# Half-width attention matmuls from one head's block, and a weight sign set on ScalarE

## The chip, the cores and the metric

The kernel runs on one core of a Trainium2 chip. The metric is the device time of one execution in microseconds (us). Three runs of the kernel before took 496.63, 497.72 and 499.42 us; the median is 497.72 us.

Engines are named as the profile names them: PE is TensorE's matmul stream and PEld its weight loads, DVE is VectorE, ACT is ScalarE, POOL is GpSimd, SP is SyncE, which here issues all DMAs.

## The reference

A linear attention over 8 batches of 8 heads, 576 positions and 64 dimensions a head, feeds a feed-forward layer with a softmax-gated unit and a layer norm:

```python
q_s = exp(q - max(q, axis=-1));  q_s /= sum(q_s, axis=-1) + 1e-09
k_s = exp(k - max(k, axis=2));   k_s /= sum(k_s, axis=2) + 1e-09
kv = einsum('bhsd,bhse->bhde', k_s, v)          # 64 x 64 for each head
x = einsum('bhsd,bhde->bhse', q_s, kv)          # -> (4608, 512)
h = x @ w_in                                     # (4608, 1024)
sm = exp(h - max(h));  sm /= sum(sm) + 1e-09
solu = h * sm
ln = (solu - mean(solu)) / sqrt(var(solu) + 1e-06) * g_ln
out = ln @ w_out                                 # (4608, 512)
```

The weights and g_ln come as 64-bit floats, w_in with 512 x 1024 and w_out with 1024 x 512 elements.

## The kernel before, in words

**Tiles.** The 4608 rows are cut into 36 row tiles of 128: each batch has 4 tiles of its 512 main rows, and the last 64 rows of two batches share one tile, called a rest tile here. A tile goes through three works: attend (`x`, kv against q gives x transposed), hidden (`h`, x against w_in, then the softmax unit) and project (`o`, against w_out). In the works' names the number is the tile's, in the tensors' names it is batch and tile of the batch: `x1_0` is batch 1, first tile.

**Two parts.** Operands of the f16 matmuls are held as a high f16 part and a low f16 part (what the high part misses). `three` (L474) multiplies high by high, high by low and low by high into one f32 accumulator. `hidden` (L515) issues 24 matmuls of 512 columns a tile at L526, `project` (L587) 24 at L600, each the same three products.

**Attention.** `keys` (L335) takes the maxima of k on DVE, turns them on PE (L322, L329), subtracts and exponentiates, and forms kv with f32 matmuls (L376, L381): 64 columns wide, alternating between the two heads of a pair, whose results lie in accumulator partitions 0 to 63 and 64 to 127. Then kv is normalised, scaled by a power of two and written into `bd` (L128): for each pair of heads a 128 x 128 block with head 0's 64 x 64 block and head 1's on the diagonal and zeros elsewhere, once for the high part (L399, ACT) and once for the low part (L401, DVE). `queries` (L441) and `rest_queries` (L463) compute q's softmax; `parts` gives the high and the low part's places in `qhl`, where each part holds all heads in a row, and a DMA transposes both into `qT`: for each part and pair a 128 x 128 block. `attend` (L493) issues, for each of 4 pairs, three matmuls of 128 x 128 weights and 128 columns (L475 to L477), 12 a tile; a rest tile has two batches' halves with 64 columns each, 24 matmuls.

**Weights.** `float_of` (L230) makes f32 from the 64-bit words: ACT scales the high word as a float (L237, Copy), DVE shifts it left by 3 and masks the sign off (L239), ors the low word's upper bits in (L241), and ors the sign of the high word in (L243). It runs eight times over 128 x 1024 elements: four for w_in (`iw`, works w0 to w3), four for w_out (`gw`, y0 to y3). The works W and Z then scale the weights to `wi` (L268, L270) and `wo` (L309, L311); `h` needs `wi`, `o` needs `wo`.

**Order.** The kernel is written as generators. `ORDER`, a long string, says which work makes its next step; a letter behind a dot (`.v`, `.p`, `.a`) moves that step to DVE, POOL or ACT. As all steps are issued in this order, the string sets each engine's queue, SP's DMA queue among them. In front stand the loads, K0, Q0, the weights and some `P` steps (`warm_up`, L648: idle matmuls on `bd[2]`).

Of the kernel before, what the change touches and what calls it, by code (L numbers as in the profile page):

```python
# [83 lines left out]
)  # L84


@with_exitstack
def linear_attention_solu_ffn(ctx: ExitStack, tc: tile.TileContext, q, k, v, w_in, w_out, g_ln, out):

# [35 lines left out]
    vr = cst.tile([P, H, D + 1], F32, name="vr")  # L125
    nc.vector.memset(vm[:, :, :, D : D + 1], 1.0)
    nc.vector.memset(vr[:, :, D : D + 1], 1.0)
    bd = [cst.tile([P, 2, NP, P], F16, name=f"bd{i}") for i in range(3)]  # L128
    for t in reversed(bd):
        nc.gpsimd.memset(t, 0.0)  # L130

# [309 lines left out]
    def queries(b, c0, c1):  # L441
# [5 lines left out]
        def parts():  # L447
            if c0 % 2 == 0:
                hl_of[b] = sb.tile([P, 2, 2, H, D], F16, name=f"qhl{b}_{c0}", tag="qhl", bufs=1)
            if n == 1:  # L450
                return (hl_of[b][:, c0 % 2, i] for i in range(2))
# [268 lines left out]
```

## Time and profile before

| what | value |
|---|---|
| median of three runs | 497.72 us |
| the profiled execution's own time | 498.03 us |
| its span, first to last instruction | 496.2 us |
| mean granted TensorE clock | 0.968 |
| `h` matmuls, L526 | 864, busy 206.0 us |
| `o` matmuls, L600 | 888, busy 197.7 us |
| `x` matmuls, L475 to L477 | 128 in each line of 128 columns, 32 in each of 64 columns |
| `kv` matmuls, L376 and L381 | 512 and 128 records |
| DMA | 74.98 MB, mean 151 GB/s |

How to read the profile: busy shares are shares of the span; the lengths of matmuls overlap, so what a matmul takes of PE's stream is read from the distance of starts. A slice row has 40 digits, each the busy share of a fortieth of the span in tenths. A row of windows gives a stretch, then for each engine its busy time and number of instructions, then the granted clock, the DMA share and GB/s. A row of groups gives line, engine, operation, tensors, shape, count, busy time and mean length of one in ns, then idle time ahead and who ended it. A row of the timeline gives start and length in us; brackets hold the idle time ahead and its releaser.

### The profile page before, as it was taken

The page shows a single profiled execution, that of the slowest core. Times are in us where ns is not written, and L with a number is a line of the kernel's source. Part 1 is how long each engine was busy: PE and PEld are TensorE (multiplying, and loading weights), DVE is VectorE, ACT ScalarE, POOL GpSimd, SP SyncE. Part 2 cuts the span into 40 slices and gives each one's busy share as a digit, 9 for nine tenths or more (in the row PEclk, how much of TensorE's full clock was granted, in tenths as well). Part 3 has the DMA queues.
Part 4 walks back from the last instruction along what each step waited for, and adds up shares of the span by engine and source line. Part 5 has one row for each costly group of instructions (what it writes and reads, how often), then busy time and mean ns, then how long its engine had stood idle before and what let it go on. Part 6 is the DMA issues. An engine that isn't in the chain of part 4 may idle for free.

```text
span 496.2 us, 8006 instructions
## 1 busy us (share of the span) xinstructions
PE 456.0 (92%) x2994; PEld 232.4 (47%) x2994; DVE 370.2 (75%) x606; ACT 278.5 (56%) x457; POOL 207.4 (42%) x305
## 2 busy tenths in 40 slices
PE   7456774999999999999999989999999999999997
PEld 2314441445554545554555444555554554444444
DVE  4999989989888679888876897779874654635330
ACT  1747588676756665684565455734764644533320
POOL 3540578358855643833276262515115320122200
PEclk9777987999999999999999999999999999999999
DMA  8596968439896599749967954684544554150532
GB/s 278 201 241 189 292 171 198 106 76 234 195 218 150 129 195 175 156 107 204 217 135 147 247 117 99 180 199 118 127 108 80 112 86 101 27 128 3 126 107 63
DMA packets 159239, 74.98 MB, mean 151 GB/s; under 512 B 127840, under 2 KB 152672, under 8 KB 159200
## 3 DMA queue, kind: packets, MB, share of 16 engines
q1 hardware_dynamic: 159200, 74.47, 65.0%
q8 instruction: 23, 0.38, 0.3%
q14 instruction: 16, 0.13, 0.1%
HBM read 36.70 MB, written 9.44 MB: 93 GB/s over the span
## 4 chain that ended last, share of the span: by engine, by line
PE 73%; DVE 19%; issue 3%; ACT 2%; DMA 1%; POOL 1%; SPq 0%; DVEq 0%; ACTq 0%; POOLq 0%
PE o L600 32%; PE h L526 32%; PE kv L376 3%; DVE u L562 2%; DVE iw L241 1%; DVE qnmx L418 1%; DMA qm<-in_q_dram 1%; PE x L475 1%; PE x L476 1%; PE x L477 1%; DVE h L555 1%; DVE wo L311 1%; DVE top L533 1%; ACT u L560 1%; DVE gw L241 1%
## 5 line engine op out<-in xcount | busy, mean ns | idle before, releaser
L526 PE MATMUL h<-wi,xT 128*128 128x512 f16 x864 | 206.0, 386 | 9.0 <-ACT e L569 8.7
L600 PE MATMUL o<-wo,uT 128*128 128x512 f16 (+1 forms) x888 | 197.7, 373 | 2.6 <-ACT os L610 1.4
L526 PEld LDWEIGHTS <-xT 128*128 128x128 f16 x864 | 84.3, 99 | 106.2 <-issue 16.2
L600 PEld LDWEIGHTS <-uT 128*128 128x128 f16 x888 | 86.2, 98 | 99.7 <-issue 3.4
L533 DVE TENSOR_REDUCE top<-h 128x1 f32<-128x1024 f32 x36 | 43.8, 1217 | 20.9 <-PE h L526 20.5
L562 DVE SCALAR_TENSOR_TENSOR u<-h,nmu,u 128x1024 f16<-128x1024 f32 x36 | 45.9, 1276 | 14.4 <-ACT u L560 14.1
L569 ACT ACTIVATE e<-h,nmu 128x1024 f32<-128x1024 f32 x36 | 39.9, 1110 | 26.7 <-DVE u L562 26.6
L555 DVE SCALAR_TENSOR_TENSOR h<-h,ph,e 128x1024 f32<-128x1024 f32 x36 | 46.4, 1289 | 8.1 <-POOL ph L552 5.2
L549 POOL TENSOR_TENSOR p<-pi,mone 128x1 f32<-128x1 f32 x36 | 23.4, 651 | 55.3 <-DVE pi L546 54.3
L535 ACT ACTIVATE nm<-top,hs 128x1 f32<-128x1 f32 x32 | 9.4, 294 | 61.0 <-DVE top L533 61.0
L543 POOL TENSOR_SCALAR am<-nm 128x1 f32<-128x1 f32 x23 | 9.5, 413 | 77.9 <-ACT nm L535 77.7
L560 ACT ACTIVATE u<-h,nmu 128x1024 f16<-128x1024 f32 x36 | 40.0, 1112 | 0.9
L539 ACT ACTIVATE e<-h,nm,hs 128x1024 f32<-128x1024 f32 x32 | 38.4, 1202 | 0.9
L608 DVE TENSOR_SCALAR os<-o,rr 128x512 f32<-128x512 f32 (+1 forms) x17 | 12.2, 717 | 31.9 <-PE o L600 31.9
L431 POOL TENSOR_TENSOR qm<-qm,qrec 128x1024 f32<-128x1024 f32 (+1 forms) x13 | 24.8, 1907 | 14.3 <-DVE qrec L429 11.3
L557 ACT ACTIVATE nmu<-s 128x1 f32<-128x1 f32 x36 | 7.3, 202 | 40.6 <-DVE h L555 39.5
L420 POOL TENSOR_TENSOR qm<-qm,qnmx 128x1024 f32<-128x1024 f32 (+1 forms) x13 | 25.6, 1969 | 8.7 <-DVE qnmx L418 8.5
L436 POOL TENSOR_TENSOR qhl<-qm,qhl 128x1024 f16<-128x1024 f32 (+1 forms) x11 | 21.6, 1963 | 17.7 <-DVE qhl L149 13.0
L511 DVE SCALAR_TENSOR_TENSOR xT<-x,xT 128x512 f16<-128x512 f32 x36 | 24.5, 680 | 4.4 <-ACT xT L509 4.3
L610 ACT ACTIVATE os<-o,rr 128x512 f32<-128x512 f32 x20 | 13.7, 685 | 23.1 <-PE o L600 13.7
L475 PE MATMUL x<-qT,bd 128*128 128x128 f16 x128 | 24.0, 225 | 2.2 <-DVE col L325 2.1
L582 POOL TENSOR_TENSOR r<-var,mhalf 128x1 f32<-128x1 f32 x36 | 20.1, 562 | 14.0 <-DVE var L579 13.2
(137 smaller groups left out, 657.4 us busy)
## 6 DMA issues: line engine op xcount, KB each, us to landing
v<-in_v_dram SPq DMA_DIRECT2D x32, 256.0 KB, 3.7
out_dram<-os SPq DMA_DIRECT2D x31, 256.0 KB, 3.4
km<-in_k_dram SPq DMA_DIRECT2D x7, 1024.0 KB, 6.9
qm<-in_q_dram SPq DMA_DIRECT2D x7, 1024.0 KB, 7.4
w_in<-in_moe_w_in_dram SPq DMA_DIRECT2D x8, 512.0 KB, 7.1
w_out<-in_moe_w_out_dram SPq DMA_DIRECT2D x8, 512.0 KB, 4.4
out_dram<-os SPq DMA_DIRECT2D x10, 128.0 KB, 2.4
km<-in_k_dram SPq DMA_DIRECT2D x2, 512.0 KB, 4.5
```

Source lines behind the costliest of these rows:

```text
L420: on(nc.gpsimd).tensor_tensor(x, x, wide(nmx), op=ALU.add)
L431: on(nc.gpsimd).tensor_tensor(x, x, wide(rec), op=ALU.mult)
L475: nc.tensor.matmul(acc, ah, bh, start=True, stop=False)
L511: nc.vector.scalar_tensor_tensor(xT[:, 1], acc, 1.0 / QS, xT[:, 0], op0=ALU.mult, op1=ALU.subtract)
L526: nc.tensor.matmul(h[:, ns], xT[:, t, kc], wi[:, s, kc, ns], start=(i == 0), stop=(i == len(terms) - 1))
L533: nc.vector.tensor_reduce(top, h, axis=AX.X, op=ALU.max, negate=True)
L539: nc.scalar.activation(e, h, AF.Exp, bias=nm, scale=hs, accum_out=z)
L555: nc.vector.scalar_tensor_tensor(h, h, ph, e, op0=ALU.mult, op1=ALU.mult, accum_out=s1)
L560: nc.scalar.activation(u[:, 0], h, AF.Identity, bias=nmu)
L562: nc.vector.scalar_tensor_tensor(u[:, 1], h, nmu, u[:, 0], op0=ALU.add, op1=ALU.subtract)
L569: nc.scalar.activation(e, h, AF.Square, bias=nmu, accum_out=s2)
L600: nc.tensor.matmul(o, uT[:, j, f], wo[:, s, f, cols], start=(f == 0 and j == 0 and s == 0), stop=(f == NF - 1 and j == 1))
```

## The change

Four things change.

1. `bd` is [128, 2, 8 heads, 64] instead of pairs of 128 x 128. For each head, slot 0 holds kv's high part in partitions 0 to 63 and again in 64 to 127 (ACT writes one half and copies it to the other), slot 1 holds the low part in partitions 0 to 63 and zeros below.
2. In `qhl` the high and the low part of one head lie side by side (64 and 64), so that the transposed `qT` holds for each head the high part in partitions 0 to 63 and the low part in 64 to 127. `attend` issues for each head two matmuls with 64 columns of weights: 16 a tile instead of 12, the two heads of a pair in turn; a rest tile has 32 instead of 24. `three` is gone.
3. The first pass of `float_of` is Prelu with a slope of -2^32 instead of Copy: a negative input comes out positive with its exponent raised by 32, which the shift by 3 turns into the sign bit. The mask and the sign pass (L243 before) are gone: two DVE passes instead of three.
4. `ORDER` is another string.

```diff
 ORDER = (
-    "LK0*4 LQ0 K0*4 LQ0 K0 P*4 K0*2 w3 Q0c w3 K0*4 V00 w3 Q0a Q0a.v V03 V00 K0.v w0*2 Q0a Q0c V01 K0 Q0b "
...
+    "LQ0*2 LK0*3 V03 w3 Q0a K0*4 Q0a*2 K0 P*4 K0 Q0b w3 V00 V03.v K0 Q0c K0 Q0b Q0a w3 w0 K0 w3 V00 Q0b "
...
-    bd = [cst.tile([P, 2, NP, P], F16, name=f"bd{i}") for i in range(3)]
+    bd = [cst.tile([P, 2, H, D], F16, name=f"bd{i}") for i in range(3)]
...
-        nc.scalar.activation(x, high.bitcast(F32), AF.Copy, scale=2.0**-112)
-        yield
-        nc.vector.tensor_scalar(xi, xi, 3, 0x7FFFFFFF, op0=ALU.logical_shift_left, op1=ALU.bitwise_and)
+        nc.scalar.activation(x, high.bitcast(F32), AF.Prelu, scale=2.0**-112, alpha=-(2.0**32))
+        yield
+        nc.vector.tensor_scalar(xi, xi, 3, -1, op0=ALU.logical_shift_left, op1=ALU.bitwise_and)
         yield
         nc.vector.scalar_tensor_tensor(xi, low, 29, xi, op0=ALU.logical_shift_right, op1=ALU.bitwise_or)
-        yield
-        nc.vector.scalar_tensor_tensor(xi, high, -0x80000000, xi, op0=ALU.bitwise_and, op1=ALU.bitwise_or)
         yield
...
+        places = t.rearrange("p s (n j) d -> p s n j d", j=2)
         for i in range(2):
-            hp = slice(i * D, (i + 1) * D)
-            nc.scalar.activation(t[hp, 0, :, hp], kvn[hp], AF.Copy, scale=s[hp])
+            hp, other = slice(i * D, (i + 1) * D), slice((1 - i) * D, (2 - i) * D)
+            high = places[:, 0, :, i]
+            nc.scalar.activation(high[hp], kvn[hp], AF.Copy, scale=s[hp])
+            yield
+            nc.scalar.copy(high[other], high[hp])
             yield
             nc.vector.scalar_tensor_tensor(
-                t[hp, 1, :, hp], kvn[hp], s[hp], t[hp, 0, :, hp], op0=ALU.mult, op1=ALU.subtract
+                places[0:D, 1, :, i], kvn[hp], s[hp], high[hp], op0=ALU.mult, op1=ALU.subtract
             )
...
-                hl_of[b] = sb.tile([P, 2, 2, H, D], F16, name=f"qhl{b}_{c0}", tag="qhl", bufs=1)
+                hl_of[b] = sb.tile([P, 2, H, 2, D], F16, name=f"qhl{b}_{c0}", tag="qhl", bufs=1)
...
-            out=qT_of[b, c0][:, cs].rearrange("p c t n k -> p (c t n) k"),
-            in_=hl_of[b][:, cs].rearrange("p c t h d -> p (c t h d)"),
+            out=qT_of[b, c0][:, cs].rearrange("p c h k -> p (c h) k"),
+            in_=hl_of[b][:, cs].rearrange("p c h t d -> p (c h t d)"),
...
             for pr in range(NP):
-                three(acc[:, pr, cols], t[:, 0, pr], t[:, 1, pr], qT[:, 0, pr, cols], qT[:, 1, pr, cols])
+
+                for s in range(2):
+                    for j in range(2):
+                        nc.tensor.matmul(
+                            acc[j * D : (j + 1) * D, pr, cols], t[:, s, 2 * pr + j], qT[:, 2 * pr + j, cols],
+                            start=(s == 0), stop=(s == 1),
+                        )
```

Three places of the new order, as the built programs hold it. First DVE's queue where `wo` is made, before:

```order
L304 TENSOR_SCALAR gs_806<-gl_69,s_out_803 128x8
L401 SCALAR_TENSOR_TENSOR bd1_81<-kvn1_698,s_kv1_759,bd1_81 64x4x64
L346 TENSOR_TENSOR khalf2_819<-km2_737 128x512
L311 SCALAR_TENSOR_TENSOR wo_68<-gw0_451,gs_806,wo_68 128x512 x2
L311 SCALAR_TENSOR_TENSOR wo_68<-gw1_480,gs_806,wo_68 128x512 x2
L311 SCALAR_TENSOR_TENSOR wo_68<-gw2_594,gs_806,wo_68 128x512
L511 SCALAR_TENSOR_TENSOR xT1_1_853<-x1_1_840,xT1_1_853 128x512
```

and the same place now:

```order
L304 TENSOR_SCALAR gs_841<-gl_69,s_out_838 128x8
L348 TENSOR_TENSOR ktop2_828<-khalf2_829 128x256
L518 SCALAR_TENSOR_TENSOR xT1_1_826<-x1_1_807,xT1_1_826 128x512
L311 SCALAR_TENSOR_TENSOR wo_68<-gw0_444,gs_841,wo_68 128x512
L346 TENSOR_TENSOR khalf2_829<-km2_736 128x512
L424 TENSOR_REDUCE qnmxr0_853<-qr0_623 128x8
L311 SCALAR_TENSOR_TENSOR wo_68<-gw0_444,gs_841,wo_68 128x512
L311 SCALAR_TENSOR_TENSOR wo_68<-gw1_504,gs_841,wo_68 128x512 x2
```

The low part of batch 1's first x (`xT1_1`) stood behind five `wo` passes and stands ahead of all now; a khalf and a row maximum of q's rest stand between the first two `wo` passes. Next PE's queue ahead of the first `o` matmul, before (`x1_0` is batch 1's first tile; the rows are the last of its 12 matmuls with their weight loads):

```order
L476 LDWEIGHTS bd1_81
L476 MATMUL x1_0_858<-qT1_0_740,bd1_81 128x128
L477 LDWEIGHTS bd1_81
L477 MATMUL x1_0_858<-qT1_0_740,bd1_81 128x128
L600 LDWEIGHTS uT0_0_562
L600 MATMUL o0_00_891<-wo_68,uT0_0_562 128x512
```

and now the same tile's 16, with what stands around them (rows that read alike are left out at the marks):

```order
L533 LDWEIGHTS xT1_1_826
L533 MATMUL h1_1_876<-wi_67,xT1_1_826 128x512
L509 LDWEIGHTS bd1_81
L509 MATMUL x1_0_885<-qT1_0_732,bd1_81 64x128
...
L533 LDWEIGHTS xT1_1_826
L533 MATMUL h1_1_876<-wi_67,xT1_1_826 128x512
...
L607 LDWEIGHTS uT0_0_569
L607 MATMUL o0_00_912<-wo_68,uT0_0_569 128x512
```

Four `h` matmuls of `h1_1` stand ahead of this tile and four behind it, and only then comes the first `o`: eight `h` matmuls moved ahead of it. Last SP's queue at the program's start, before:

```order
L181 DMA km0_97<-in_k_dram 128x4x256 x2
L200 DMA kr0_100<-in_k_dram 64x8x64
L181 DMA qm0_102<-in_q_dram 128x4x256 x2
L227 DMA w_in3_139<-in_moe_w_in_dram 128x1024 x2
L187 DMA v0_0_153<-in_v_dram 128x2x256
```

and now:

```order
L182 DMA qm0_97<-in_q_dram 128x4x256 x2
L182 DMA km0_100<-in_k_dram 128x4x256 x2
L201 DMA kr0_103<-in_k_dram 64x8x64
L188 DMA v0_3_105<-in_v_dram 128x2x256
L228 DMA w_in3_107<-in_moe_w_in_dram 128x1024 x2
```

q's two halves now go ahead of k's, and one block of v ahead of the first weights.

More of the change, by code (lines that the diff above doesn't have):

```diff
@@ L448, in parts @@
             if c0 % 2 == 0:
-                hl_of[b] = sb.tile([P, 2, 2, H, D], F16, name=f"qhl{b}_{c0}", tag="qhl", bufs=1)
+                hl_of[b] = sb.tile([P, 2, H, 2, D], F16, name=f"qhl{b}_{c0}", tag="qhl", bufs=1)
             if n == 1:
-                return (hl_of[b][:, c0 % 2, i] for i in range(2))
-            return (hl_of[b][:, :, i].rearrange("p c h d -> p h c d") for i in range(2))
+                return (hl_of[b][:, c0 % 2, :, i] for i in range(2))
+            return (hl_of[b][:, :, :, i].rearrange("p c h d -> p h c d") for i in range(2))
         yield from q_softmax(x[:, :, 0] if n == 1 else x, parts, H * n, f"{b}_{c0}")
         if c0 % 2 == 0:
-            qT_of[b, c0] = sb.tile([P, 2, 2, NP, P], F16, name=f"qT{b}_{c0}", tag="qT", bufs=2)
+            qT_of[b, c0] = sb.tile([P, 2, H, P], F16, name=f"qT{b}_{c0}", tag="qT", bufs=2)
             qT_of[b, c0 + 1] = qT_of[b, c0]
         nc.sync.dma_start_transpose(
-            out=qT_of[b, c0][:, cs].rearrange("p c t n k -> p (c t n) k"),
-            in_=hl_of[b][:, cs].rearrange("p c t h d -> p (c t h d)"),
+            out=qT_of[b, c0][:, cs].rearrange("p c h k -> p (c h) k"),
+            in_=hl_of[b][:, cs].rearrange("p c h t d -> p (c h t d)"),
         )
@@ L464, in parts @@
         def parts():
-            hl_of["rest"] = sb.tile([P, 2, H, D], F16, name=f"qhlr{b}", tag="qhlr", bufs=1)
-            return (hl_of["rest"][:, i] for i in range(2))
+            hl_of["rest"] = sb.tile([P, H, 2, D], F16, name=f"qhlr{b}", tag="qhlr", bufs=1)
+            return (hl_of["rest"][:, :, i] for i in range(2))
         yield from q_softmax(raw["qr"], parts, H, f"r{b}")
-        qT = qT_of["rest", b // 2] = sb.tile([P, 2, NP, P], F16, name=f"qTr{b}", tag="qTr", bufs=1)
+        qT = qT_of["rest", b // 2] = sb.tile([P, H, P], F16, name=f"qTr{b}", tag="qTr", bufs=1)
         nc.sync.dma_start_transpose(
-            out=qT.rearrange("p t n k -> p (t n) k"), in_=hl_of["rest"].rearrange("p t h d -> p (t h d)")
+            out=qT, in_=hl_of["rest"].rearrange("p h t d -> p (h t d)")
         )
-    def three(acc, ah, al, bh, bl):
-        nc.tensor.matmul(acc, ah, bh, start=True, stop=False)
-        nc.tensor.matmul(acc, ah, bl, start=False, stop=False)
-        nc.tensor.matmul(acc, al, bh, start=False, stop=True)
     xT_of, uT_of, r_of, hs_of = {}, {}, {}, {}
@@ L648, in warm_up @@
     def warm_up():
-        idle = bd[2][:, 0].rearrange("p n k -> p (n k)")
+        idle = bd[2][:, 0].rearrange("p h d -> p (h d)")
         while True:
@@ L654, in warm_up @@
             for _ in range(4):
-                nc.tensor.matmul(acc, bd[2][:, 0, 0], idle, start=True, stop=True)
+                nc.tensor.matmul(acc, idle[:, 0:P], idle, start=True, stop=True)
             yield
```

124 rows, old and new, of the table ORDER are left out of this document.

## The prediction

> **What bounds the kernel now.** I read the page's busy rows and the two slice rows first, then the windows of two stretches, then the timeline where the one stretch passes into the other.
>
> ```profile
> span 496.2 us, 8006 instructions
> PE 456.0 (92%) x2994; PEld 232.4 (47%) x2994; DVE 370.2 (75%) x606; ACT 278.5 (56%) x457; POOL 207.4 (42%) x305
> PE   7456774999999999999999989999999999999997
> DVE  4999989989888679888876897779874654635330
> ...
> 10.00:92.00 82.00, 51.33 (x377) 27.50 (x378) 78.08 (x109) 57.47 (x88) 44.22 (x41) 0.81 0.78 218
> 92.00:493.00 401.00, 397.51 (x2597) 202.43 (x2596) 287.97 (x488) 219.55 (x368) 159.82 (x256) 1.00 0.63 136
> ```
>
> The 92% of PE is an average over two kernels in one. From 10 to 92 us PE works 51 of 82 us and DVE 78.1 of 82: DVE's queue is the clock there. From 92 to 493 us PE is busy 397.5 of 401 us at a granted clock of 1.00, and DVE 288: PE is the clock. So an edit is worth what it takes off DVE's queue in the first stretch and off PE's stream in the second; anything else must only not be late.
>
> ```profile
> 89.73 5.04 DVE L311 SCALAR_TENSOR_TENSOR wo<-gw,gs,wo 128x512 f16<-128x512 f32 x5
> 91.16 0.38 PE L600 MATMUL o<-wo,uT 128*128 128x512 f16 x1
> 92.17 2.58 PE L600 MATMUL o<-wo,uT 128*128 128x512 f16 x11 [0.63 <-DVE wo L311]
> ```
>
> This is the hand-over: the first `o` matmuls start at 91.16 and then wait for DVE's second `wo` pass. From there PE runs to the end, so the kernel ends when the second `wo` pass is done plus PE's remaining stream.
>
> **First stretch: DVE's queue ahead of the second wo pass.** The change takes the sign pass away (L243, eight times), since ScalarE's pass sets the sign. The new order also carries other passes across this point. Counted in the order of both kernels, up to the second `wo` pass: gone are the eight sign passes, one half-size qm+qnmx and one qhl subtraction. New are two copies into vm, one half-size cast, one khalf, one ktop, one km-kb, two full qm·qrec and one half-size one, one xT, and three 128x1 passes.
>
> ```profile
> L243 DVE SCALAR_TENSOR_TENSOR iw<-w_in,iw 128x1024 int32<-128x1024 int32 x4 | 4.9, 1225 | 0.1
> L243 DVE SCALAR_TENSOR_TENSOR gw<-w_out,gw 128x1024 int32<-128x1024 int32 x4 | 4.8, 1216 | 0.0
> L420 DVE TENSOR_TENSOR qm<-qm,qnmx 128x512 f32<-128x512 f32 x1 | 2.0, 1983 | 0.0
> L436 DVE TENSOR_TENSOR qhl<-qm,qhl 128x1024 f16<-128x1024 f32 x6 | 7.6, 1271 | 0.3 <-ACT qhl L147 0.3
> ...
> L149 DVE COPY vm<-v x4: 414/654/2317, 195.7 to 346.7; 128x512 f32<-128x512 f32 x4
> L149 DVE CAST qhlr<-qr 128x512 f16<-128x512 f32 x1 | 0.4, 417 | 0.0
> L346 DVE TENSOR_TENSOR khalf<-km 128x512 f32<-128x512 f32 x16 | 13.2, 826 | 4.6 <-DMA km<-in_k_dram 4.3
> L348 DVE TENSOR_TENSOR ktop<-khalf 128x256 f32<-128x256 f32 x16 | 8.1, 505 | 0.3
> L357 DVE TENSOR_TENSOR km<-km,kb 128x1024 f32<-128x1024 f32 x8 | 10.7, 1337 | 2.2 <-ACT kb L332 2.2
> L431 DVE TENSOR_TENSOR qm<-qm,qrec 128x1024 f32<-128x1024 f32 x4 | 4.9, 1220 | 0.1
> L511 DVE SCALAR_TENSOR_TENSOR xT<-x,xT 128x512 f16<-128x512 f32 x36 | 24.5, 680 | 4.4 <-ACT xT L509 4.3
> L552 DVE TENSOR_TENSOR ph<-p,hs 128x1 f32<-128x1 f32 x14 | 3.9, 278 | 3.1 <-POOL p L549 3.1
> ```
>
> Gone: 4 x 1.225 + 4 x 1.216 = 9.76, with 1.98 and 1.27 more it is 13.0 us. New: 2 x 0.65 (the median of the vm copies; their ends are 0.41 and 2.32) + 0.42 + 0.83 + 0.51 + 1.34 + 2 x 1.22 + 0.61 (half of 1.22) + 0.68 + 3 x 0.28 = 9.0 us. **Net -4.0 us.** With the copies at 0.41 it is -4.5, at 2.32 it is -0.7; were all of what moved hidden, the sign passes alone would give -9.8. I take -4.0, since DVE has no idle time here that could swallow it.
>
> ScalarE's pass is Prelu instead of Copy; its length is not in the trace. The two nearest rows, L237's own and Exp over the same size, bound it at 1.05 to 1.13 us; as ScalarE is busy 57 of 82 us, that is nothing. The copy that each head half of kv now makes on ScalarE is not in the trace either: between nothing and the 0.50 us of L399, which handles the same 64x256; I take 0.5. Two stand ahead of each batch's first `x`. DVE's low pass waits only for the activation ahead of each copy, as before, so one copy at most lies on the path to `x`; PE's `h` and `o` of the batch before cover it. With that cover gone it would be 0.5 us in each of 8 batches, 4 us.
>
> ```profile
> L237 ACT ACTIVATE gw<-w_out 128x1024 f32<-128x1024 f32 x4 | 4.5, 1126 | 0.0
> L422 ACT ACTIVATE qm<-qm 128x1024 f32<-128x1024 f32 x15 | 15.8, 1053 | 1.0 <-POOL qm L420 1.0
> L399 ACT ACTIVATE bd<-kvn,s_kv 64x256 f16<-64x256 f32 x16 | 8.0, 500 | 1.8 <-DVE s_kv L167 1.6
> ...
> 4.61 0.69 DVE L346 TENSOR_TENSOR khalf<-km 128x512 f32<-128x512 f32 x1 [3.63 <-DMA km<-in_k_dram]
> 7.64 0.69 DVE L351 TENSOR_TENSOR ktop<-ktop,kr 64x512 f32<-64x512 f32 x1
> 10.30 1.81 DVE L418 TENSOR_REDUCE qnmx<-qm 128x16 f32<-128x1024 f32 x2 [0.48 <-DMA qm<-in_q_dram]
> ```
>
> SP now issues q's two halves ahead of k's. Before, the first load is in at 4.6 us and all five (k, kr, q) at 10.3. So kr, fifth now, comes at about 10.3 instead of 7.6, and DVE's k maxima end up to 2.6 us later. In return the first qnmx runs at 4.6, and POOL and ScalarE do their part of q while DVE waits. Bounds 0 and +2.6; I take **+0.5**, nearer to the covered end, as DVE was idle for most of these ten microseconds anyway.
>
> **Second stretch: PE's stream.** A tile of `x` was 12 matmuls of full width; it becomes 16 of half width, in two column halves. The trace has no such f16 matmul, but `kv` (L376) is of that form: 64 columns, the two halves in turn.
>
> ```profile
> 119.86 0.22 PE L475 MATMUL x<-qT,bd 128*128 128x128 f16 x1
> ...
> 120.53 1.03 PE L526 MATMUL h<-wi,xT 128*128 128x512 f16 x4
> 121.48 1.15 PE L376 MATMUL kv<-vm,km 128*64 128x65 f32 x32
> 122.57 0.60 PE L526 MATMUL h<-wi,xT 128*128 128x512 f16 x2
> ...
> 139.17 0.19 PE L475 MATMUL x<-qTr,bd 128*128 128x64 f16 x1
> ...
> 139.87 0.22 PE L475 MATMUL x<-qT,bd 128*128 128x128 f16 x1
> ...
> 160.45 1.03 PE L526 MATMUL h<-wi,xT 128*128 128x512 f16 x4
> 161.41 2.09 PE L376 MATMUL kv<-vm,km 128*64 128x65 f32 x64
> 163.43 1.04 PE L526 MATMUL h<-wi,xT 128*128 128x512 f16 x4
> ...
> 257.04 5.18 PE h L526 x24
> ...
> 344.10 0.64 PE L322 MATMUL turned<-ident,ktop 128*128 128x128 f32 x4
> 344.57 1.24 PE L600 MATMUL o<-wo,uT 128*128 128x512 f16 x5
> ```
>
> By starts, not by lengths (they overlap): an `h` matmul takes 5.18 / 24 = 0.216 us of the stream, a tile of `x` 120.53 - 119.86 = 0.67, a tile of rest rows 0.70 (its 24 matmuls move 64 columns each). Four `h` from 120.53 on would end at 121.39, yet the next one starts at 122.57: 32 `kv` matmuls cost 1.18. In the same way the run of 64 costs 163.43 - 161.31 = 2.12. The difference gives 0.94 / 32 = 0.0294 us each, and **0.24 us for every run** however long, for going into the half-width form and out. The 0.0294 also says that the halves overlap: an f32 transpose of 128 columns takes 0.47 / 4 = 0.118 us, so 65 f32 columns alone would need some 0.06, twice what `kv` takes.
>
> An `x` tile alone will thus take 16 x 0.0294 + 0.24 = 0.71 (was 0.67), two in one run 1.18 (was 1.34), a rest tile 32 x 0.0294 + 0.24 = 1.18 (was 0.70). Behind the first `o` stand 26 tiles and 4 rest tiles in both orders; there the new order has 37 runs of half-width matmuls, the old one 14 (`kv` alone). Before: 26 x 0.67 + 4 x 0.70 = 20.2. After: 544 x 0.0294 + 23 x 0.24 = 21.5: **+1.3 us**. PE also does eight `h` matmuls ahead of the first `o` that stood behind it: 8 x 0.216 = **-1.7**; the second `wo` pass ends four passes, some 3 us, behind their xT, and PE needs 1.7 + 0.7 for these and an `x`, so they cost the hand-over nothing. Bounds: with rest pairs at 0.029 instead of 0.059 us -1.9 more; without overlap +10.9 (below).
>
> The Trainium skill's page TensorEngine Tiling (Array Packing), Key Properties, says that a change of tiling mode drains the array; the trace agrees with 0.24 us a run, and without it the sum would be 5.5 us lower. Its Performance and Restrictions parts add that column tiling shuts off the fast weight load; by that rule a rest pair cannot keep the full-width pitch of 0.029 us that rest rows have now, which speaks for the 0.059 taken.
>
> **The sum.** -4.0 + 0.5 + 1.3 - 1.7 = -3.9 us on the profiled execution's 498.0 us (span 496.2 and 1.8 around it): 494.1. The median of the runs shown, 497.7, is 0.06% below that, so I say **494.0**.
>
> **Rivals.**
> *The gain is swallowed in the first stretch* (about 498). What is late next is the chain from `u` of the first tile to the third tile's top:
>
> ```profile
> 64.01 7.03 PE L526 MATMUL h<-wi,xT 128*128 128x512 f16 x24 [2.33 <-ACT e L569]
> ```
>
> The third tile's `h` must wait for ScalarE's square to free its accumulator, and then takes 7.0 us where a run of 24 takes 5.2 later. DVE had just enough other passes to fill that; with a sign pass fewer in between, DVE would wait there and at the other chains instead. For it speaks that DVE was idle only 4 us in 82, so fillers count; against it, that passes of q and kr were moved in. If all 3.9 us go, 498.0.
>
> *The halves don't overlap in f16* (slower). Place: every `x` tile of the second stretch. Then 16 matmuls run one behind the other at the 0.67 / 12 = 0.056 us of a full-width one: 26 x 16 x (0.0556 - 0.0294) = 10.9 us more, 505. It decides once a pair takes over 0.078 us (3.9 us over 26 x 8 pairs, on 0.059). `kv`'s pitch speaks against it, but that is f32, where the trace holds two matmuls for each that is written.
>
> *More than forecast* (about 489): the second stretch's 3.5 us of PE idle time go as well and rest pairs run at the full-width pitch, 1.9 us.
>
> *The new order makes PE wait in the second stretch* (over 500). There DVE and ScalarE work 288 and 220 of 401 us, so it takes an unlucky order, with over 6 us of waits.
>
> That Prelu needs a table of its own can be left out: the changed order has one table load on ScalarE, as before.
>
> **The numbers.** Forecast 0.50 (491 to 496), swallowed 0.24 (496 to 500), no overlap 0.12 (505), more 0.08 (487 to 490), waits in the second stretch 0.06 (over 500). Half a per cent, 2.5 us, is about what a measurement can tell from none. Faster by more (below 495.2): 0.47 of the forecast's 0.50 and the 0.08, 0.55. Within: 0.25. Slower (above 500.2): 0.12 + 0.06 + 0.02 from the swallowed case's edge, 0.20. The range 487 to 502 leaves out the case without overlap and part of the last.
>
> **What would show it.** Right: the first `o` at about 87.5 us; DVE over 90% busy up to there; `x` runs of 0.7 us from the last full-width start to the next; rest tiles near 1.2; PE idle under 6 us behind. Wrong: the first `o` still past 90 us with DVE waiting for PE or ScalarE (swallowed); `x` matmuls with starts 0.056 us apart throughout (no overlap); waits of `h` or `o` over 6 us in sum (order).

## The result, and the profile after

The changed kernel took 491.12 us (median of four runs, 489.83 to 491.42) beside 498.57 us for the kernel before on the same chip: a ratio of 0.985, interval 0.981 to 0.989. Run again later it took 493.42 us (median of six, 490.94 to 496.84), ratio 0.990, interval 0.987 to 0.994. Both lie in the range forecast, on the fast side of 494.0. The profiled execution took 489.83 us, 8.2 us less than that of before. What made it up is not what the prediction said.

From the page of the changed kernel, the span, the busy rows and the slices of PE and DVE:

```profile
span 488.0 us, 8325 instructions
PE 453.0 (93%) x3150; PEld 223.0 (46%) x3150; DVE 359.2 (74%) x610; ACT 280.2 (57%) x463; POOL 202.7 (42%) x303
PE   5748576999999999999999999999999999999997
DVE  3989999987889897887897885987786754544220
```

The shape is the same: DVE sets the pace of the first seven slices, PE that of the rest. The windows of the two stretches say it with numbers. The first row reaches from the start to the end of DVE's second `wo` pass; its counterpart of before follows below:

```profile
0.00:87.66 87.66, 58.62 (x424) 28.28 (x425) 74.95 (x124) 59.31 (x90) 37.40 (x44) 0.84 0.89 234
...
10.00:87.80 77.80, 52.58 (x408) 26.47 (x409) 73.10 (x117) 57.33 (x88) 33.15 (x34) 0.82 0.90 232
88.00:484.00 396.00, 393.49 (x2724) 194.31 (x2722) 283.44 (x486) 220.56 (x373) 164.92 (x260) 1.00 0.60 137
```

```profile
0.00:92.78 92.78, 59.11 (x400) 30.28 (x401) 82.66 (x121) 59.73 (x91) 47.74 (x50) 0.83 0.79 221
```

Up to the end of the second `wo` pass DVE works 74.95 us instead of 82.66, so 7.7 us less, and idles 12.7 instead of 10.1, so 2.6 us more: the pass ends 5.1 us earlier. The place of the hand-over, DVE's timeline first and then PE's:

```profile
85.05 0.75 DVE L311 SCALAR_TENSOR_TENSOR wo<-gw,gs,wo 128x512 f16<-128x512 f32 x1
...
86.92 4.19 DVE L311 SCALAR_TENSOR_TENSOR wo<-gw,gs,wo 128x512 f16<-128x512 f32 x5
```

```profile
86.40 0.64 PE L509 MATMUL x<-qT,bd 128*64 128x128 f16 x16
86.97 1.04 PE L533 MATMUL h<-wi,xT 128*128 128x512 f16 x4
87.84 2.75 PE L607 MATMUL o<-wo,uT 128*128 128x512 f16 x12
```

The second `wo` pass, the first of the five from 86.92, is done at 87.66, and PE comes to its first `o` at 87.84: the twelve go through without the wait that stood there before. That wait was for another pass than the prediction said. By the loop of `project`, the second of the twelve matmuls reads DVE's first `wo` pass and the fifth reads its second. Before the change the second matmul waited, for the first pass, which took 2.39 us (0.74 is usual) beside a pass of POOL:

```profile
89.28 2.29 POOL L420 TENSOR_TENSOR qm<-qm,qnmx 128x1024 f32<-128x1024 f32 x1
```

```profile
89.73 2.39 DVE L311 SCALAR_TENSOR_TENSOR wo<-gw,gs,wo 128x512 f16<-128x512 f32 x1
```

It ended at 92.12, the matmul started at 92.17, and the second pass, done at 92.78, was just in time for the fifth at 92.83. In what follows "the first `o`" is the start of that group, and "the rest" is the span less that start: 405.1 us before, 400.2 now.

PE's waits behind the hand-over, in order of cost, before (92 to 493 us) and after (88 to 484 us); the columns are total, times and longest:

```profile
PE o L600 <- ACT os L610: 1.4, 1, 1.4
PE h L526 <- ACT e L569: 0.7, 2, 0.4
PE o L600 <- DVE wo L311: 0.6, 1, 0.6
PE o L600 <- DVE os L608: 0.6, 2, 0.4
PE h L526 <- DVE xT L511: 0.2, 1, 0.2
```

```profile
PE h L533 <- ACT e L576: 1.7, 3, 0.9
PE o L607 <- DVE os L615: 0.8, 1, 0.8
```

Added up, 3.5 us became 2.5. The prediction had left this term as it was.

### The profile page after: what moved, and what is told of

It reads as the page before. It is cut to its first block, busy times and chain, and to the rows that moved or that the text cites. A ratio compares the mean times of both kernels' runs of the same rounds, so it can differ in the third digit from the quotient of the medians.

```text
span 488.0 us, 8325 instructions
## 1 busy us (share of the span) xinstructions
PE 453.0 (93%) x3150; PEld 223.0 (46%) x3150; DVE 359.2 (74%) x610; ACT 280.2 (57%) x463; POOL 202.7 (42%) x303
## 4 chain that ended last, share of the span: by engine, by line
PE 78%; DVE 12%; ACT 4%; DMA 3%; issue 2%; SPq 0%; POOL 0%; DVEq 0%; ACTq 0%
PE o L607 36%; PE h L533 34%; PE x L509 3%; PE kv L376 3%; DMA kr<-in_k_dram 2%; DVE u L569 2%; DVE top L540 1%; DMA v<-in_v_dram 1%; DVE wi L270 1%; ACT u L567 1%; DVE gw L243 1%; DVE h L562 1%; ACT e L576 1%; DVE qnmx L424 1%; PE kv L381 1%
## 5 line engine op out<-in xcount | busy, mean ns | idle before, releaser
L533 PE MATMUL h<-wi,xT 128*128 128x512 f16 x864 | 203.9, 385 | 11.2 <-ACT e L576 9.8
L533 PEld LDWEIGHTS <-xT 128*128 128x128 f16 x864 | 84.2, 99 | 111.6 <-issue 18.5
L442 POOL TENSOR_TENSOR qhl<-qm,qhl 128x1024 f16<-128x1024 f32 (+1 forms) x12 | 24.9, 2075 | 34.9 <-ACT qhl L148 22.0
L550 POOL TENSOR_SCALAR am<-nm 128x1 f32<-128x1 f32 x17 | 7.6, 449 | 70.0 <-ACT nm L542 69.9
L509 PEld LDWEIGHTS <-bd 128*64 128x64 f16 x640 | 18.3, 113 | 15.7 <-issue 11.6
```

What stands on the lines that cost most here:

```text
L442: on(nc.gpsimd).tensor_tensor(lo, x, hi, op=ALU.subtract)
L509: nc.tensor.matmul(acc[j * D : (j + 1) * D, pr, cols], t[:, s, 2 * pr + j], qT[:, 2 * pr + j, cols], start=(s == 0), stop=(s == 1),)
L533: nc.tensor.matmul(h[:, ns], xT[:, t, kc], wi[:, s, kc, ns], start=(i == 0), stop=(i == len(terms) - 1))
```

## The experiments

Three edits were made at once: the sign set by ScalarE (**sign**), the half-width `x` from one head's block (**attend**), and the new order (**order**). The first four kernels do one or two of them on the kernel before, the next two undo one of them in the changed kernel, so that all eight combinations have a time.

### Sign alone

```diff
-        nc.scalar.activation(x, high.bitcast(F32), AF.Copy, scale=2.0**-112)
+        nc.scalar.activation(x, high.bitcast(F32), AF.Prelu, scale=2.0**-112, alpha=-(2.0**32))
...
-        nc.vector.tensor_scalar(xi, xi, 3, 0x7FFFFFFF, op0=ALU.logical_shift_left, op1=ALU.bitwise_and)
+        nc.vector.tensor_scalar(xi, xi, 3, -1, op0=ALU.logical_shift_left, op1=ALU.bitwise_and)
...
-        nc.vector.scalar_tensor_tensor(xi, high, -0x80000000, xi, op0=ALU.bitwise_and, op1=ALU.bitwise_or)
```

The rest is the kernel before, with its order; the removed pass leaves its empty step.

> The kernel before, its order too, with the Prelu pass and without the eight sign passes (an empty step stands in their place). Queue theory: DVE's queue ahead of the second wo pass is 9.8 us shorter and nothing is moved in, so the first o starts 8 to 9.8 us earlier, near 82 us, and the time is about 489. Rival (chains): DVE waits for PE, ScalarE and POOL instead, the first o starts at 87 or later, and the time is 494 or more; DVE's waits between 10 us and the first o grow from 2 to over 5 us.

490.98 us beside 498.02, ratio 0.986 (0.982 to 0.989). This one edit is worth as much as the whole change. PE's timeline at the hand-over, and DVE's waits from 10 to 83 us:

```profile
83.21 0.38 PE L599 MATMUL o<-wo,uT 128*128 128x512 f16 x1
84.24 2.58 PE L599 MATMUL o<-wo,uT 128*128 128x512 f16 x11 [0.65 <-DVE wo L310]
```

```profile
DVE xT L510 <- ACT xT L508: 1.2, 1, 1.2
DVE g L294 <- ACT junk_out L286: 1.1, 1, 1.1
DVE qnmx L417 <- DMA qm<-in_q_dram: 1.1, 2, 0.8
```

The first `o` starts 8.0 us earlier (83.21, was 91.16) for 9.76 us of passes taken away; the rest stays, 405.2. Up to its second `wo` pass DVE works 10.6 us less than before and idles 2.7 us more. DVE's waits for ScalarE in the first two rows, which the kernel before does not have in this stretch, are the larger part of that idle time: the swallowing that the first rival spoke of exists, but it takes 1.8 of 9.8 us net, a fifth, not all.

### Attend alone

The new `bd`, `qhl`, `qT` and `attend` in the old order. That order has no step for the copy, so it is issued with the activation:

```diff
             nc.scalar.activation(high[hp], kvn[hp], AF.Copy, scale=s[hp])
-            yield
             nc.scalar.copy(high[other], high[hp])
             yield
```

> The kernel before, its order too, with the new attend, bd, qhl and qT (the copy on ScalarE in the same step as the activation). Stream theory, with the lengths of the changed kernel's trace (0.66 us for an x tile alone, 0.72 for a rest tile): the second stretch is 0 to 2.5 us shorter, the first o starts within 0.5 us of 91.2; time 496 to 498.5. Rival: the added copies are on the path, up to 4 us: time 500 or more. Rival: all of the gain sits here: 491.

497.35 us beside 498.02, ratio 0.998 (0.996 to 1.000): a gain of a few tenths of a per cent at most is all that this can say. The profile has the first `o` at 91.58 and a rest of 405.2 us, both as before.

### Sign and attend in the old order

> Both edits in the order of before. If the edits carry the gain and add up: the sum of the two runs with one edit each, 486 to 489. If the new order carries it: 495 or more.

488.98 us, ratio 0.981 (0.978 to 0.985), the lowest of all.

```profile
84.02 0.38 PE L606 MATMUL o<-wo,uT 128*128 128x512 f16 x1
85.29 2.58 PE L606 MATMUL o<-wo,uT 128*128 128x512 f16 x11 [0.90 <-DVE wo L311]
```

The first `o` starts at 84.02, earlier than in the changed kernel, and the rest takes 402.6. Beside attend alone, measured together with it, sign is worth 8.4 us here.

### Order alone

The old code in the new order, in which the step of the copy is empty and the sign pass is issued with the low word's pass.

> The new order with neither edit (the sign pass is issued in the low pass's step). Queue theory: the passes moved ahead of the second wo pass cost DVE 9.0 less 3.25, so 5.7 us, and the eight h matmuls moved ahead give back 1.7: the first o at about 97, the time 500 to 503. Rival (the order is the gain): 491 to 494.

500.70 us beside 498.02, ratio 1.0045 (1.0027 to 1.0063): slower, and by an interval that leaves 1 out.

```profile
97.64 2.75 PE L601 MATMUL o<-wo,uT 128*128 128x512 f16 x12
```

The first `o` comes 6.5 us later than before. The count of passes on record gives nearly that (9.0 moved in less 3.25 moved out, and 0.5 for the loads, is 6.3), but the trace has another sum: up to the second `wo` pass DVE works 2.8 us more and idles 2.0 more, so that the pass ends 4.8 us later; the other 1.7 is that the first `o` started 1.6 us ahead of that pass's end in the old order and 0.1 behind it here. The near agreement is luck. The rest is shorter, 400.8 for 405.1, but 4.3 doesn't pay for 6.5.

### The changed kernel without sign

```diff
-        nc.scalar.activation(x, high.bitcast(F32), AF.Prelu, scale=2.0**-112, alpha=-(2.0**32))
+        nc.scalar.activation(x, high.bitcast(F32), AF.Copy, scale=2.0**-112)
         yield
-        nc.vector.tensor_scalar(xi, xi, 3, -1, op0=ALU.logical_shift_left, op1=ALU.bitwise_and)
+        nc.vector.tensor_scalar(xi, xi, 3, 0x7FFFFFFF, op0=ALU.logical_shift_left, op1=ALU.bitwise_and)
         yield
         nc.vector.scalar_tensor_tensor(xi, low, 29, xi, op0=ALU.logical_shift_right, op1=ALU.bitwise_or)
+        nc.vector.scalar_tensor_tensor(xi, high, -0x80000000, xi, op0=ALU.bitwise_and, op1=ALU.bitwise_or)
```

> The changed kernel with the eight sign passes back (issued in the low pass's step). Queue theory: the whole 9.8 us come back: first o at 97 to 98, time about 500.5. Rival (chains, sign passes only fill waits): under 496.

500.56 us beside 499.1, ratio 1.0035 (1.0018 to 1.0053): without sign the change would be a loss.

```profile
98.39 2.75 PE L608 MATMUL o<-wo,uT 128*128 128x512 f16 x12
```

The first `o` is 10.6 us later than the changed kernel's 87.84, and the rest is the same 400.2. So all that sign does is done ahead of the first `o`.

### The changed kernel without attend

`bd`, `qhl`, `qT` and `attend` as before the change, the step of the copy empty.

> The changed kernel with the old attend, bd, qhl and qT. Stream theory: first o within 0.5 us of 87.8, and 0.67 us for each x tile in place of 0.66 alone or 1.09 for two in one run: second stretch 1 to 2.5 us longer, time 492 to 494. Rival (attend is neutral or a loss): 491 or less.

493.16 us beside 499.1, ratio 0.990 (0.983 to 0.996), with the first `o` at 88.42 and a rest of 400.8. The interval holds the changed kernel's own ratio, so the time alone doesn't settle the worth of attend. The rest, 400.8 against 400.2, puts it at 0.6 us in this order; the changed kernel's rest was 400.2 in both of its profiles.

### The eight combinations

Ratios to the kernel before, measured together with each, and the two parts of the profiled span:

| sign | attend | order | ratio (interval) | first `o` | the rest |
|---|---|---|---|---|---|
| | | | 1 | 91.2 | 405.1 |
| x | | | 0.986 (0.982 to 0.989) | 83.2 | 405.2 |
| | x | | 0.998 (0.996 to 1.000) | 91.6 | 405.2 |
| x | x | | 0.981 (0.978 to 0.985) | 84.0 | 402.6 |
| | | x | 1.0045 (1.0027 to 1.0063) | 97.6 | 400.8 |
| | x | x | 1.0035 (1.0018 to 1.0053) | 98.4 | 400.2 |
| x | | x | 0.990 (0.983 to 0.996) | 88.4 | 400.8 |
| x | x | x | 0.985 (0.981 to 0.989) | 87.8 | 400.2 |

Sign is worth 1.4 to 1.9% wherever it is added. Attend is worth 0.1 to 0.5% by the medians, but in no pair are the intervals apart; in the traces it takes 0 to 2.6 us off the rest, in part through PE's waits, below. Order costs 0.4 to 0.6% in each of the four pairs; the intervals are apart in the two pairs without sign and overlap in the two with it. In the profile order moves the first `o` back by 3.8 to 6.8 us and shortens the rest by 2.4 to 5.0.

### The halves apart

All matmuls of one column half, then all of the other:

```diff
-            for pr in range(NP):
-
-                for s in range(2):
-                    for j in range(2):
+            for j in range(2):
+                for pr in range(NP):
+                    for s in range(2):
```

> The changed kernel with attend's loops turned, so that one column half's eight matmuls are issued before the other half's eight. If only neighbours in different halves overlap: 16 x 0.0556 + 0.24 = 1.13 us a tile and about as much for a rest tile, against 0.66 and 0.72: 26 x 0.47 + 4 x 0.41 = 13.9 us in the second stretch, time about 505. If PE finds the other half by itself: 491.

497.49 us beside 499.1, ratio 0.997 (0.995 to 0.999). PE's timeline around one tile of `x`, here and in the changed kernel:

```profile
149.62 1.24 PE L606 MATMUL o<-wo,uT 128*128 128x512 f16 x5
150.79 0.89 PE L508 MATMUL x<-qT,bd 128*64 128x128 f16 x16
151.61 0.82 PE L606 MATMUL o<-wo,uT 128*128 128x512 f16 x3
```

```profile
146.26 1.24 PE L607 MATMUL o<-wo,uT 128*128 128x512 f16 x5
147.43 0.64 PE L509 MATMUL x<-qT,bd 128*64 128x128 f16 x16
148.00 0.82 PE L607 MATMUL o<-wo,uT 128*128 128x512 f16 x3
```

Five `o` at 0.216 us would end at 150.70 and 147.34; the tile then takes 151.61 - 150.70 = 0.91 us apart and 0.66 us in turn. So issuing the halves in turn is worth 0.25 us a tile, but it isn't all that lets them overlap: apart, a tile would need 16 x 0.056 + 0.21 = 1.1 us if nothing did. By the single starts of this tile, the first five and the last five matmuls stand some 0.06 us apart, the seven steps between 0.028. In a run of two tiles the second adds 0.51 us (0.45 in turn). The rest grew by 5.6 us to 405.8: 18 tiles alone by 0.25, four runs of two by 0.31 and four rest tiles by 0.20 make 6.5, and PE's waits, by its starts, were 0.9 less (2.1 us, 3.0 in the changed kernel). The first `o` was also 2.3 us later, at 90.12; k's second load landed 1.4 us later in this run (last section), and the tiles of `x` ahead of the hand-over are longer too.

### k's loads first again

The changed kernel with one piece of its order turned back: `LK0*3 LQ0*2` in front instead of `LQ0*2 LK0*3`.

> The changed kernel with k's loads ahead of q's, as before. If the load order costs the 0.5 us that the prediction takes: 490.6, first o 0.5 earlier. Bounds: up to 2.6 us earlier, or up to 2 us later, if the q part that runs while k loads is what fills DVE.

492.82 us beside 499.1, ratio 0.990 (0.986 to 0.993); first `o` at 91.44, which is later, where an earlier one was to be tested. DVE's timeline at the start shows why:

```profile
10.33 0.69 DVE L424 TENSOR_REDUCE qnmx<-qm 128x8 f32<-128x512 f32 x1 [9.35 <-DMA qm<-in_q_dram]
```

DVE's queue still began with q's maximum, so it stood for 9.35 us; k's maxima then followed without a wait. The experiment turned back the loads without the queue that they feed and says nothing about the loads alone; a miss of its design.

### Both versions once more

Sign and attend in the old order, and the changed kernel, on one chip with more runs.

> Both edits in the order of before, once more, beside the changed kernel on one chip. If the new order is a loss with the edits in: 488 to 490, some 2 us below the changed kernel of this call, first o 3 to 4 us earlier and a second stretch 2 to 3 us longer. If that difference was the chip's: equal within 1 us.

> The changed kernel beside it: 490 to 492; first o at 87 to 88.5, second stretch 396.7.

491.25 us (488.13 to 491.64, five runs) and 493.42 us (490.94 to 496.84, six), ratios 0.985 (0.982 to 0.988) and 0.990 (0.987 to 0.994). The old order is ahead by 2.2 us, with intervals that still overlap; the first time their medians were 2.1 us apart, but were not measured together. The profiles have the first `o` at 83.76 and 88.98, and the rest is 402.6 and 400.2 as in the first ones: the old order is 5.2 us better ahead of the first `o` and 2.4 us worse behind it. By the medians the best version tried is thus both edits in the old order, by some 2 us. An order with the old first stretch and the new second one wasn't tried.

## Why the prediction came out near, and where it was wrong

The sum on record was -3.9 us; the profiled executions differ by -8.2, the medians by -7.5 in the first runs and -5.4 in the later ones. That the time fell near the forecast is in part luck, as the errors of the terms have both signs:

| term | forecast | measured |
|---|---|---|
| DVE's work up to the second `wo` pass | -4.0 | -7.7 |
| DVE's idle time up to there (the loads) | +0.5 | +2.6 |
| `x` behind the first `o` | +1.3 | -1.0 |
| eight `h` moved ahead | -1.7 | -1.7 |
| PE's other waits | 0 | -1.5 |
| from that pass to the `o` matmul that reads it, and rounding | 0 | +1.1 |

The third to the fifth term are sums over the starts of all of PE's matmuls: behind its first `o` PE stood 5.3 us before, of which 0.8 was the wait at the hand-over, and 3.0 now.

**What bounds each stretch: right in the main, wrong at the hand-over.** DVE's 73.1 of 77.8 us before the hand-over, PE's 393.5 of 396 behind it and the unchanged rest in the experiment without sign bear out that an edit is worth what it takes off the queue that sets the pace. But the prediction let PE wait for DVE's second `wo` pass. Before the change it waited for the first, whose 2.39 us the row of five (5.04 us) hid. In the changed kernel it waited for neither. PE's timeline:

```profile
76.92 4.99 PE L533 MATMUL h<-wi,xT 128*128 128x512 f16 x12 [4.04 <-ACT e L576]
82.02 0.32 PE L154 MATMUL wide_out<-ident,m_out 128*128 128x128 f32 x1
```

From 76.92 to the first `o` PE never stands for more than 0.1 us. Those twelve `h` start 0.43 us apart at a granted clock of 0.50 (77 to 81 us), where 0.216 is the distance at 1.00; then come `wide_out`, 20 more `h` and two tiles of `x`. The fifth `o`, which reads the second `wo` pass, starts at 88.70, and the pass was done at 87.66. So the first `o` at 87.84 (87.5 was named) was set by PE's own queue, and the step that failed is that the eight `h` cost the hand-over nothing: they stand in that queue. The pass would have let the fifth `o` start 1.0 us earlier, so by these times moving them was worth about 0.7 of the 1.7 us; that is an estimate, as no run moved them alone.

**DVE's work: the direction right, the size off by 3.7 us.** The step took every pass at the mean of its group and assumed that means carry over. Groups by line of DVE, before and after:

```profile
L239 DVE TENSOR_SCALAR gw<-gw 128x1024 int32<-128x1024 int32 x4 | 4.3, 1078 | 0.3 <-ACT gw L237 0.3
L239 DVE TENSOR_SCALAR iw<-iw 128x1024 int32<-128x1024 int32 x4 | 4.3, 1068 | 0.0
```

```profile
L241 DVE TENSOR_SCALAR gw<-gw 128x1024 int32<-128x1024 int32 x4 | 2.8, 688 | 0.4 <-ACT gw L239 0.4
L241 DVE TENSOR_SCALAR iw<-iw 128x1024 int32<-128x1024 int32 x4 | 2.7, 672 | 1.1 <-ACT iw L239 1.1
L559 DVE TENSOR_TENSOR ph<-p,hs 128x1 f32<-128x1 f32 x1 | 2.3, 2317 | 0.0
```

The shift pass, which was taken as unchanged, lost 3.1 us over eight: 8.6 became 5.5. The first `wo` pass lost 1.6 (2.39 became 0.75). The other way, a `ph` pass of one element a partition, priced at 0.28, took 2.32. The edit of the shift's instruction isn't the cause: with the new one in the old order (sign alone) `iw`'s four still take 4.4 us, and with the old one in the new order (order alone) 2.7. What stands beside a pass on POOL changed, as the last section shows.

**The loads: mis-sized in the first stretch.** 0.5 us was chosen near the covered end of 0 to 2.6. DVE's timeline:

```profile
6.13 0.69 DVE L424 TENSOR_REDUCE qnmx<-qm 128x8 f32<-128x512 f32 x1 [5.15 <-DMA qm<-in_q_dram]
8.00 0.69 DVE L346 TENSOR_TENSOR khalf<-km 128x512 f32<-128x512 f32 x1 [1.18 <-DMA km<-in_k_dram]
10.30 0.69 DVE L346 TENSOR_TENSOR khalf<-km 128x512 f32<-128x512 f32 x1 [1.16 <-DMA km<-in_k_dram]
...
11.57 0.68 DVE L351 TENSOR_TENSOR ktop<-ktop,kr 64x512 f32<-64x512 f32 x1
```

The first q half is there at 6.1, not at the 4.6 of the first k half before, and the last of k's maxima ends at 12.25 instead of 8.33. DVE idles 5.15 + 1.18 + 1.16 = 7.5 us up to there, by its timeline; in the kernel before it idled 5.6 us over the same passes. So 1.9 of the 2.6 us stand at the loads, in this profile; the other 0.7 stand later. "DVE was idle for most of these ten microseconds anyway" was no reason: idle time that was there before hides nothing new, and the upper part of the range was the better choice.

**`x`: mis-sized, and of the wrong sign.** Two tiles in one run and a rest tile of the changed kernel, from PE's timeline:

```profile
109.65 0.81 PE L607 MATMUL o<-wo,uT 128*128 128x512 f16 x3
110.39 1.08 PE L509 MATMUL x<-qT,bd 128*64 128x128 f16 x32
111.41 0.82 PE L607 MATMUL o<-wo,uT 128*128 128x512 f16 x3
...
200.72 1.46 PE L533 MATMUL h<-wi,xT 128*128 128x512 f16 x6
202.11 0.69 PE L509 MATMUL x<-qTr,bd 128*64 128x64 f16 x32
202.74 1.04 PE L533 MATMUL h<-wi,xT 128*128 128x512 f16 x4
```

Two tiles take 111.41 - 110.30 = 1.11 (forecast 1.18), one alone 0.66 (0.71): so 0.45 for 8 pairs, 0.056 a pair, and 0.21 for a run. A rest tile takes 202.74 - 202.02 = 0.72 where 1.18 was forecast: 0.51 / 16 = 0.032 a pair. The price of `kv` was carried over as if the moved columns did not count. It fitted main tiles by the luck of the sizes: one `kv` record, with 65 f32 columns, takes 0.029 us, and one matmul of a main pair, with 128 f16 columns, 0.028. A rest pair moves 64 f16 columns and took little more than half of a main pair. With these three prices the formula on record gives 208 x 0.056 + 64 x 0.032 + 23 x 0.21 = 18.5 us; summed over every tile of the trace it is 19.2, before it was 20.2. The low bound on record ("-1.9 more") was the right one, and the sentence drawn from the Trainium skill against it, from TensorEngine Tiling (Array Packing), Restrictions, that column tiling shuts off the fast weight load, isn't borne out by time here: a pair of half-width matmuls takes nearly the 0.029 us that one full-width matmul of rest rows had. The drain at a change of mode, of Key Properties on the same page, is: 0.21 us a run.

**PE's waits: taken as unchanged, -1.5.** The waits changed hands: `o` waits less for its own evacuation, `h` more for ScalarE. It isn't settled by which edit. Attend in the old order without sign stands 6.0 us and with it 3.8, on the same program behind the hand-over; only the time at which the work gets there differs.

**The rivals.** Swallowed: a fifth, as sign alone shows. No overlap: not so, and from the same price on which it stood, 0.056 a pair against 0.078 to decide. More than forecast: half of it came true, the rest pairs, and one of 3.5 us of waits. An order that makes PE wait: no, 2.5 us; but there was a case that none of them named, an order that loses ahead of the hand-over more than it saves behind it. The forecast had a number for it, +5.75 us of passes moved in (order alone measured 2.8, and 2.0 of idle time), and summed it with the sign passes into one -4.0. Had it been shown as a term of its own, the question whether the order is worth having would have stood there.

ScalarE's parts went nearly as bounded: Prelu 1145 and 1153 ns against Copy's 1126, just past the 1.05 to 1.13 given, and the copy 403 ns of at most 500.

## What to carry to other kernels

Where a change has several parts, price each as a term with its own sign: a sum that comes out right can hold a part that should be left away, as the new order here, which costs 2 to 3 us by the medians. A pass removed from the engine that sets the pace was worth nearly its length here (8.0 of 9.8 us). Where two queues reach a hand-over within a microsecond of each other, as DVE's and PE's did, say for both when they get there: the later one sets it. A price taken from a row of another type or width should stand at both ends of its range in the sum before one is chosen.

## What was not expected of the hardware

**A DVE pass can be held for as long as a POOL pass runs.** From the timelines of the changed kernel, POOL and DVE:

```profile
60.19 2.36 POOL L357 TENSOR_TENSOR km<-km,kb 128x1024 f32<-128x1024 f32 x1
```

```profile
60.43 3.19 DVE L243 SCALAR_TENSOR_TENSOR gw<-w_out,gw 128x1024 int32<-128x1024 int32 x1
```

A pass that takes 1.22 us elsewhere starts 0.24 us behind POOL's and ends at 63.62, 1.07 us behind POOL's end at 62.55. In the kernel before the same shows at another place:

```profile
67.69 1.90 POOL L431 TENSOR_TENSOR qm<-qm,qrec 128x1024 f32<-128x1024 f32 x1
```

```profile
67.88 2.26 DVE L239 TENSOR_SCALAR gw<-gw 128x1024 int32<-128x1024 int32 x1 [0.27 <-ACT gw L237]
```

A pass of 0.68 us elsewhere ends at 70.14, 0.55 us behind POOL's end at 69.59. The `ph` pass above and the first `wo` pass at the hand-over of before fell beside a pass of POOL in the same way. Not every pass is held: the row maximum at 59.31 in the changed kernel, beside POOL's pass from 58.33 to 60.23, took its usual 1.21 us. The Trainium skill's page SBUF — State Buffer, SBUF: two separate sides, tells of a port pair that the two engines share for some of DVE's operations, and that the first to start holds for its whole instruction, while the other waits; both places agree. No run here took POOL's pass away, so this is read from the traces and not tested. It would explain why the means of DVE's groups changed with the order alone.

**The first stretch varies from run to run, the second doesn't in these profiles.** PE's time from its first `o` to its last matmul was 396.7 us in the changed kernel's profiles and in those of the versions without sign and with k first; with both edits in the old order it was 399.1 twice. But the second half of k's block let DVE start at 10.30 us in the first profile, at 11.09 when the kernel was run again, and at 11.73 in the version with the halves apart, whose program is the same up to there; the first `o` came at 87.84, 88.98 and 90.12. The two sets of runs of the changed kernel differ by 2.3 us in their medians. What makes a load land later wasn't found.
